# Both exponentials of a batch together, consumers later, four h banks and a shorter prologue in a fused attention and snake kernel

## Chip, cores, metric

One core of a Trainium2 chip. Times are device microseconds (us) of a whole execution; a profile's span, from its first to its last instruction, is 1.5 to 2 us shorter. The kernel before takes 348.2 us (median of three runs, 345.6 to 351.0).

## The reference

```python
# attention part: x (8, 8, 512, 64), state (8, 8, 32, 64), B, H, S, D = x.shape
a  = softmax(x @ state^T / sqrt(D));      xread = a  @ state   # (8, 8, 512, 64)
a2 = softmax(state @ x^T / sqrt(D));      sread = a2 @ x       # (8, 8,  32, 64)
h_in = concat([xread, sread], axis=2) -> (4352, 512)
# MoE part: w_in (512, 2048), w_out (2048, 512), alpha (2048)
h = h_in @ w_in;  s = sin(alpha * h);  g = h + s * s / (alpha + 1e-9);  out = g @ w_out
```

## The kernel before

A pass `t` has 16 slots `f`, one for each 128 rows of the hidden layer. A slot makes `h` of batch `t` (`mm1`: 2 matmuls, a sine on ScalarE, its square on GpSimd; in pass 0 every second square is on VectorE), finishes the slot before it (`snake` on VectorE: `g = h + s2 / alpha`), does a quarter of an output tile of batch `t-1` (`mm2`: 4 matmuls), and one step of the attention of batch `t+1` (the list `fill`). Pass 8 treats the state rows. M is state times w_in, so that `h = A @ M`. There are eight PSUM banks: 3 for h, 2 for the output, 3 (`psX`, "px") for all the rest.

```python
psH = tile_pool(name="psH", bufs=3, PSUM); psO = (bufs=2); psX = (bufs=3)
...
load_x(0, 2); ... w_in (4 loads); load_x(1, 1); w_out (4 loads)
for b in range(2, B):
    load_x(b, 1)                      # all issued by GpSimd (POOL) at the start
...
def s_step(ii):                       # scores of two of four row blocks, and their exponential
    ... 8 matmuls into sp ...
    nc.scalar.activation(a.E[:, 2*ii:2*ii+2, :], sp[:], ACT.Exp, scale=scale)
def r_step(ii):                       # row sums, reciprocal (VectorE); normalise (GpSimd)
    nc.vector.reduce_sum(R, E8, axis=AX.X); nc.vector.reciprocal(rR, R)
    nc.gpsimd.tensor_tensor(A8, E8, rR..., ALU.mult)
def a_step(): ...                     # transposes of A; copy to AT (needed by mm1 of the next pass)
...
return [lambda: t_step(0),            # pack (VectorE) and transposes of x
        lambda: t_step(1), lambda: s_step(0),
        lambda: (s_step(1), r_step(0)), lambda: r_step(1), None, a_step]
...
fill = [an[0], an[1], an[2], an[3], an[4], mn[0], an[6]] + mn[1:]   # mn: eight M steps
fill = fill + w_steps(t)              # W and C (the state rows' attention): slots 14, 15
for f in range(FT):
    cur = mm1(t, f)
    if fill[f]: fill[f]()
    if pend: snake(*pend)             # one slot behind
    pend = (t, f) + cur
    if t > 0: mm2(t - 1, f // 4, (f % 4) * 4, (f % 4) * 4 + 4, box)
```

The softmax here doesn't subtract the row's maximum and nothing guards it: scores larger than these inputs give would overflow.

## Time and profile before

| | before |
|---|---|
| time, us | 348.2 (345.6 to 351.0) |
| TensorE busy, share of the span | 78% |
| mean granted TensorE clock | 0.879 |
| table loads on ScalarE | 30, of 1.28 us |
| prologue / t=0 / passes t=1..6 / rest, us | 33.4 / 33.9 / 226.1 / 54.3 |

The last row cuts the span at the first transposes of a batch, the group whose output is `x_ps`; the rest is t=7, t=8 and the last output tiles. The lines are in the prediction. The clock of the prologue is not to be trusted: the profile gives 1.00 there, before the first change that it recorded.

### The profile page before, as it was taken

To read this page: it belongs to the slowest core of one execution; us is meant where nothing else is said; L and a number is where in the kernel's file an instruction comes from. 1 tells how busy PE (TensorE), PEld (TensorE's weight loads), DVE (VectorE), ACT (ScalarE), POOL (GpSimd) and SP (SyncE) were. 2 spreads that over 40 slices of the span, in tenths; PEclk is the share of its full clock that TensorE was granted. 3 is DMA by queue.
4 is the path that set the end of the run, shared out by engine and by line. 5 is a ranking of instruction groups with operands and counts; after the bars stand their busy time and mean duration, and the time that the engine had idled before them with its cause. 6 is when DMAs were issued, how large, how long until landed. Compare 5 with 4: busy or idle time off the path is not lost.

```text
span 347.7 us, 4220 instructions
## 1 busy us (share of the span) xinstructions
PE 269.5 (78%) x1536; PEld 119.7 (34%) x1536; DVE 178.1 (51%) x285; ACT 174.5 (50%) x256; POOL 165.3 (48%) x176
## 2 busy tenths in 40 slices
PE   2515478695997689776979599749978699999993
PEld 1302222342343233332334234313333235445651
DVE  3522666744466346754565355744654466654320
ACT  1212955266452935384635745493528464564431
POOL 8433342226462465345552646345534556785420
PEclk9999855587898969996998789987989699999998
DMA  8999960000000000000110000000000001011112
GB/s 105 206 203 203 197 83 1 2 1 31 30 32 30 30 32 30 30 2 30 38 55 0 31 30 32 30 31 32 30 32 1 30 32 61 30 62 53 38 62 61
DMA packets 19780, 17.84 MB, mean 51 GB/s; under 512 B 2992, under 2 KB 15280, under 8 KB 19760
## 3 DMA queue, kind: packets, MB, share of 16 engines
q0 software_dynamic: 12704, 8.65, 16.7%
q1 hardware_dynamic: 7056, 8.92, 7.3%
q8 instruction: 12, 0.20, 0.3%
q14 instruction: 8, 0.07, 0.1%
HBM read 17.31 MB, written 8.91 MB: 75 GB/s over the span
## 4 chain that ended last, share of the span: by engine, by line
PE 56%; ACT 15%; DVE 9%; issue 7%; POOL 6%; DMA 5%; ACTq 0%; POOLq 0%
PE o_ps L309 30%; PE h_ps L282 13%; ACT L293 5%; DMA w_out_sb<-in_moe_w_out_dram 5%; PE m_ps L218 5%; ACT L176 4%; ACT s L293 4%; PE x_ps L158 3%; POOL A L185 3%; DVE xp L146 3%; DVE gT L300 2%; PE h_ps L288 2%; DVE rC L264 2%; PE a_ps L193 2%; ACT o_sb L315 1%
## 5 line engine op out<-in xcount | busy, mean ns | idle before, releaser
L296 POOL TENSOR_TENSOR s<-s 128x512 bf16<-128x512 bf16 (+1 forms) x136 | 134.2, 989 | 153.0 <-ACT s L293 147.3
L293 ACT ACTIVATE s<-h_ps,alpha_sb 128x512 bf16<-128x512 f32 (+1 forms) x144 | 94.9, 664 | 118.6 <-PE h_ps L282 107.7
L309 PE MATMUL o_ps<-w_out_sb,gT 128*128 128x512 bf16 x544 | 149.3, 402 | 0.0
L300 DVE SCALAR_TENSOR_TENSOR gT<-s,inva_sb,h_ps 128x512 bf16<-128x512 bf16 (+1 forms) x144 | 100.7, 705 | 37.3 <-POOL s L296 36.4
L282 PE MATMUL h_ps<-AT,M 128*128 128x512 bf16 x256 | 87.2, 426 | 20.6 <-DVE gT L300 20.6
L309 PEld LDWEIGHTS <-gT 128*128 128x128 bf16 x544 | 49.2, 102 | 56.1 <-issue 19.6
L282 PEld LDWEIGHTS <-M 128*128 128x128 bf16 x256 | 25.8, 104 | 57.2 <-issue 34.8
L228 DVE CAST M<-m_ps 128x512 bf16<-128x512 f32 x32 | 22.0, 687 | 34.3 <-PE m_ps L218 34.3
L315 ACT COPY o_sb<-o_ps 128x512 f32<-128x512 f32 x34 | 19.9, 584 | 21.4 <-PE o_ps L309 20.9
L218 PE MATMUL m_ps<-w_in_sb,stT 128*64 128x512 bf16 x128 | 29.9, 479 | 0.2 <-ACT M L226 0.2
L193 PE MATMUL a_ps<-ident,A 128*128 128x128 bf16 x64 | 9.5, 301 | 24.8 <-POOL A L185 24.8
L158 PE MATMUL x_ps<-ident,xp 128*128 128x128 bf16 x128 | 13.2, 265 | 19.7 <-DVE xp L146 19.7
L226 ACT CAST M<-m_ps 128x512 bf16<-128x512 f32 x32 | 18.6, 580 | 13.5 <-PE m_ps L218 13.5
L183 DVE TENSOR_REDUCE R<-E 128x16 f32<-128x512 bf16 x16 | 11.0, 684 | 26.7 <-ACT E L176 26.6
L158 PEld LDWEIGHTS <-xp 128*128 128x128 bf16 x128 | 10.5, 121 | 27.1 <-DVE xp L146 24.4
L176 ACT ACT_TABLE_LOAD x15 | 19.2, 1283 | 1.0 <-PEq L378 0.7
L163 DVE COPY xT<-x_ps 128x1024 bf16<-128x1024 bf16 x16 | 11.1, 691 | 16.5 <-PE x_ps L158 16.5
L293 ACT ACT_TABLE_LOAD x15 | 19.2, 1283 | 0.3
L185 POOL TENSOR_TENSOR A<-E,rR 128x512 bf16<-128x512 bf16 x16 | 16.9, 1059 | 4.3 <-DVE rR L184 4.3
L218 PEld LDWEIGHTS <-stT 128*64 128x64 bf16 x128 | 7.6, 115 | 31.1 <-issue 30.9
L193 PEld LDWEIGHTS <-A 128*128 128x128 bf16 x64 | 6.3, 134 | 30.4 <-POOL A L185 27.5
L176 ACT ACTIVATE E<-s_ps 128x512 bf16<-128x512 f32 x16 | 9.4, 597 | 13.5 <-PE s_ps L170 13.3
(33 smaller groups left out, 110.7 us busy)
## 6 DMA issues: line engine op xcount, KB each, us to landing
out_dram<-o_sb SPq DMA_DIRECT2D x32, 256.0 KB, 2.2
xnat<-in_x_dram POOLq DMA_DIRECT2D x7, 512.0 KB, 21.2
w_in_sb<-in_moe_w_in_dram POOLq DMA_DIRECT2D x4, 512.0 KB, 10.2
w_out_sb<-in_moe_w_out_dram POOLq DMA_DIRECT2D x4, 512.0 KB, 19.2
xnat<-in_x_dram POOLq DMA_DIRECT2D x2, 256.0 KB, 5.5
out_dram<-o_sb SPq DMA_DIRECT2D x8, 64.0 KB, 1.7
st_nat<-in_state_dram POOLq DMA_DIRECT2D x1, 256.0 KB, 4.5
alpha_sb<-in_moe_alpha_dram SPq DMA_DIRECT2D x1, 8.0 KB, 3.1
```

Of the source, the lines that this page charges most:

```text
L158: nc.tensor.transpose(tp[:, k, i * P:(i + 1) * P], a.xp[:, i, 2 * q:2 * q + 2, :].rearrange("p r d -> p (r d)"), ident[:],)
L176: nc.scalar.activation(a.E[:, 2 * ii:2 * ii + 2, :], sp[:], ACT.Exp, scale=scale)
L185: nc.gpsimd.tensor_tensor(A8, E8, rR.unsqueeze(2).to_broadcast([P, 2 * H, Ns]), ALU.mult)
L193: nc.tensor.transpose(tp[:, g, i * P:(i + 1) * P], a.A[:, i, g * P:(g + 1) * P], ident[:],)
L218: nc.tensor.matmul(mp[k * 2 * Ns:(k + 1) * 2 * Ns, :], stT[:, b * G + g, k * 2 * Ns:(k + 1) * 2 * Ns], w_in_sb[:, q, fs * FW:(fs + 1) * FW ...
L228: nc.vector.tensor_copy(dst, mp[:])
L282: nc.tensor.matmul(hp[:, :n], Ms[t][:, g, f * P:(f + 1) * P], atts[t].AT[:, g, :], start=(g == 0), stop=(g == G - 1),)
L293: nc.scalar.activation(s[:, :n], hp[:, :n], ACT.Sin, scale=alpha_sb[:, f:f + 1])
L296: eng.tensor_tensor(s2[:, :n], s[:, :n], s[:, :n], ALU.mult)
L300: nc.vector.scalar_tensor_tensor(gT[t][:, f, :n], s2[:, :n], inva_sb[:, f:f + 1], hp[:, :n], ALU.mult, ALU.add)
L309: nc.tensor.matmul(op[:], gT[t][:, ft, st * P:(st + 1) * P], w_out_sb[:, ft, :], start=(ft == 0), stop=(ft == FT - 1),)
L315: nc.scalar.copy(o_sb[:], op[:])
```

## The change

Its intent is to keep TensorE from waiting in a pass, and to start earlier. The exponentials of a batch stand together (two table loads a pass instead of four); their consumers come some slots later; four h banks and a snake two slots behind give slack; W and C move from slots 14 and 15 to 6 and 7; the pack moves from slot 0 to the end of the slot before it; inputs of later batches are loaded two passes ahead instead of all at the start; the state is transposed with half the matmuls; twelve matmuls on zeros are to warm the clock. In pass 0 all squares go to GpSimd and all copies of M to ScalarE, and W and C share one bank. In the diff, T are the transposes of x, S the scores, X the exponential, Rs the row sums and reciprocal, N the normalisation, AT_ the transposes of A; the pack is the copy of x into `xp` that T needs.

```diff
-    psH bufs=3 ... psX bufs=3          (sinp bufs=3)
+    psH bufs=4 ... psX bufs=2          (sinp bufs=4)
-    for b in range(2, B):
-        load_x(b, 1)
... (prologue)
+    warm_up(12)
     prep_state()                        # 16 transposes of doubled columns instead of 32
+    a.S(0); a.X(0); a.S(1); a.X(1); <load the sine table>; a.Rs(0); a.N(0, nc.gpsimd)
+    a.Rs(1); a.N(1, nc.vector); m_step(0, 0..3, True); a.AT_([0]); a.AT_([1])
+    m_step(0, 4..7, True); atts[1] = Att(1); atts[1].pack(0, 1)
... (a pass)
-        fill = [an[0], an[1], an[2], an[3], an[4], mn[0], an[6]] + mn[1:]
+            add(pe, 0, n.T, 0);  add(pe, 1, n.T, 1)
+            add(pe, 3, n.S, 0);  add(pe, 4, n.S, 1)
+            add(post, 4, n.X, 0); add(post, 4, n.X, 1)
+            add(post, 7, n.Rs, 0)
+            add(post, 8, n.N, 0, nc.gpsimd); add(post, 8, n.Rs, 1)
+            add(post, 9, n.N, 1, nc.gpsimd)
+            add(pe, 12, n.AT_, [0, 1])
+            for k, s in enumerate((2, 8, 9, 10, 11, 13, 14, 15)):
+                add(pe, s, m_step, t + 1, k, t == 0 or k % 2 == 0)
+            s = 6 if t + 1 < B else 0
+            add(pe, s, atts[t].W); add(pe, s + 1, atts[t].Cs)
+            add(post, 5, load_x, t + 2, 1)
+            add(post, 15, nxt)            # pack of batch t + 2
-        eng = nc.vector if (t == 0 and f % 2) else nc.gpsimd; eng.tensor_tensor(s2 ...)
+        nc.gpsimd.tensor_tensor(s2 ...)
-            if pend: snake(*pend)
+            pend.append((t, f) + cur)
+            if len(pend) > LAG: snake(*pend.pop(0))      # LAG = 2
```

`pe` work goes ahead of the slot's snake and mm2, `post` work behind them. A half batch is now four heads of all rows instead of all heads of half the rows, which changes no size.

## The prediction

> **What bounds the kernel now.** I read the page's forty slices first, then the windows table cut at the kernel's own stages, then the timeline of one steady period and of the start.
>
> ```profile
> PE   2515478695997689776979599749978699999993
> ...
> PEclk9999855587898969996998789987989699999998
> ```
>
> TensorE (PE) is the busiest engine, but it has dips at regular distances, and in the same slices the granted clock falls to 5 to 8 tenths. So there is a periodic hole, and after each hole TensorE runs slowly. I cut the span where the first transposes of a batch start (the x_ps group of the timeline): 33.4, 67.3, 106.9, ... 257.2, and at 293.4, where t=7 begins, which has none. The columns are: stretch, its length, then busy us (instructions) of PE, PEld, DVE, ACT, POOL, then the clock, DMA share and GB/s.
>
> ```profile
> 0.00:33.40 33.40, 11.15 (x90) 6.20 (x91) 12.02 (x26) 5.79 (x8) 17.05 (x26) 1.00 1.18 178
> 33.40:67.32 33.92, 23.07 (x113) 8.26 (x113) 22.04 (x38) 19.82 (x28) 11.54 (x11) 0.62 0.59 80
> ...
> 182.10:220.20 38.10, 31.38 (x177) 13.43 (x178) 20.66 (x31) 20.96 (x30) 18.55 (x18) 0.87 0.08 28
> ...
> 293.40:347.70 54.30, 48.55 (x269) 24.99 (x266) 22.04 (x37) 23.24 (x42) 26.42 (x32) 0.98 0.16 54
> ```
>
> These are the prologue (33.4 us), the pass t=0 (33.9), one of the six steady passes t=1..6 (67.3 to 293.4 us, so 226.1 in all, 37.7 each), and t=7, t=8 and the drain (54.3). In a steady pass TensorE is busy 31.4 of 38.1 us at clock 0.87; ACT, DVE and POOL are at about 21, 21 and 19 us, none near the bound. In the last stretch TensorE is 48.6 of 54.3 busy at 0.98. So TensorE bounds the end, and in the steady passes it is TensorE plus holes and cold clock. The holes, from the timeline (start, length, engine, line; in brackets idle before and what ended it):
>
> ```profile
> 180.51 1.53 DVE L146 COPY xp<-xnat 128x2048 bf16<-128x2048 bf16 x1
> ...
> 182.10 1.03 PE L158 MATMUL x_ps<-ident,xp 128*128 128x128 bf16 x8 [2.51 <-DVE xp L146]
> ...
> 187.99 1.28 ACT L176 ACT_TABLE_LOAD   x1
> ...
> 189.29 0.60 ACT L176 ACTIVATE E<-s_ps 128x512 bf16<-128x512 f32 x1
> ...
> 189.90 1.28 ACT L293 ACT_TABLE_LOAD   x1
> ...
> 191.90 1.28 ACT L176 ACT_TABLE_LOAD   x1
> ...
> 193.20 0.60 ACT L176 ACTIVATE E<-s_ps 128x512 bf16<-128x512 f32 x1
> ...
> 194.29 1.28 ACT L293 ACT_TABLE_LOAD   x1
> ...
> 194.72 0.66 DVE L300 SCALAR_TENSOR_TENSOR gT<-s,inva_sb,h_ps 128x512 bf16<-128x512 bf16 x1
> 195.43 1.01 PE L282 MATMUL h_ps<-AT,M 128*128 128x512 bf16 x2 [2.01 <-DVE gT L300]
> ...
> 198.44 0.82 PE L193 MATMUL a_ps<-ident,A 128*128 128x128 bf16 x6 [1.79 <-POOL A L185]
> ```
>
> The first pair: the transposes of the next batch waited 2.51 us for its pack copy. The rest: ScalarE (ACT) switches table four times, 1.28 us each, because each of the two exponentials stands between sines; the sines come late, h banks come free late (TensorE idle 2.01 us for gT), and then the a_ps transposes wait 1.79 us for POOL's normalisation. Idle here is 38.10 - 31.38 = 6.7 us. At the start:
>
> ```profile
> 16.91 0.88 POOL L77 DMA_DIRECT2D xnat<-in_x_dram  x1 [1.66 <-DMA w_in_sb<-in_moe_w_in_dram]
> ...
> 22.11 0.88 POOL L77 DMA_DIRECT2D xnat<-in_x_dram  x1 [1.74 <-DMA xnat<-in_x_dram]
> ...
> 27.19 0.87 POOL L77 DMA_DIRECT2D xnat<-in_x_dram  x1 [1.67 <-DMA w_out_sb<-in_moe_w_out_dram]
> 28.08 2.06 POOL L185 TENSOR_TENSOR A<-E,rR 128x512 bf16<-128x512 bf16 x2
> ...
> 30.20 0.82 PE L193 MATMUL a_ps<-ident,A 128*128 128x128 bf16 x6 [0.60 <-POOL A L185]
> ```
>
> POOL is stuck issuing input loads: each of the last ones waits for an older transfer, 2.5 us apart, so POOL's first normalisation starts only at 28.08, and everything else waits for it.
>
> **What the Trainium skill says.** "TensorE: Matmul & The Clock Gate", Part 1 and "HAM oscillation": half rate by default, full rate after some 3.4 us of sustained work, back to half after an idle window of that length. The trace agrees in kind: in 1 us windows the clock was 0.50 from 182 to 185 and back at 1.00 by 186, after a hole of 2.5 us, so the hole can be shorter than the page's rule; after the same hole at 217.7 it did not fall.
> "ScalarE: Activation LUTs", What ACT_TABLE_LOAD costs: about 1283 ns, plus a drain, about 2.66 us a switch. The trace agrees on 1283 ns but shows no drain: sine and table load, and load and exponential, follow each other within 0.02 us. I use 1.28.
> "PSUM — Partial Sum Buffer", Specifications: 8 banks. Both kernels use all: 3+2+3 before, 4+2+2 after.
> "SBUF — State Buffer", Who interferes with whom: copies in VectorE's two-port mode and GpSimd block each other. The trace fits: the same 128x2048 pack copy took 0.68 us at 32.7 us, between POOL instructions, and 1.53 beside them. I use 1.5 in a steady pass.
>
> **The change, part by part.**
> *Dense cost of a steady pass.* The TensorE work is unchanged. Of the chain of waits, one slot (mm1 2 matmuls, mm2 4) takes 1.30 us when dense (300 to 320 us) and 1.74 with an M step (92 to 98 us). From distances in the timeline at full clock: a group of x transposes 0.46, a group of eight scores 0.23, A transposes 0.46 (estimated as eight x transposes), all W 0.46, C 0.34. Sum: 16 x 1.30 + 8 x 0.44 + 2 x 0.46 + 2 x 0.23 + 0.46 + 0.46 + 0.34 = 20.8 + 3.5 + 2.6 = 27.0 us. Against 38.1 there are 11.1 us to win: 6.7 idle, and 0.13 x 38.1 = 5.0 of clock.
> *Both exponentials together.* Two table loads instead of four. Take the end of mm1 of slot 4 as zero: sine at 0.8, load 2.1, exponentials 2.7 and 3.3, load 4.6, sine 5 at 5.3, its square on POOL at 6.4, snake at 7.2. With four h banks mm1 of slot 9 is the first to need that snake. Slots 5 to 8 give TensorE 4 x 1.3 plus W 0.46, C 0.34 and an M step 0.44, plus the rest of slot 4, so it comes there at about 7.5: hidden, just. VectorE then has in a row C's reciprocal and products (0.96 + 0.59), snakes, two reductions with reciprocals (2 x 0.94) and M copies; snake 6 ends near 9.7 against 9.2 wanted. I take 0.8 us of stalls here.
> *Consumers later.* The normalisations are in slots 8 and 9, A transposes in slot 12: by the same count POOL ends at 12.7, TensorE arrives at 13.5. The 1.8 us wait goes.
> *Pack.* The new order puts the pack behind the M copy and snake of slot 15, and its transposes into the next slot. From the end of the last M matmul: copy 0.8, snake 1.55, pack 3.1; TensorE has mm2 0.86 and mm1 0.43, so it waits 1.8 us. The hole shrinks from 2.5 but stays.
> *Clock.* One 1.8 us hole and some small ones; I allow a fall after a third of the holes, 3.3 us at half rate, and a little more: 0.6 us. Sum of a pass: 27.0 + 0.8 + 1.8 + 0.6 = 30.2, I take 30.
> *t=0.* There is no mm2 to cover the table loads. From the first T: TensorE at half rate for slots 0 to 4 (5 x 0.85 + T, S and one M step) about 7 us; sine 5 is ready 5.3 later and slot 9 starts 7.2 later, at about 14; from there POOL sets the pace with seven squares and two normalisations at 1.05, and the last M steps and pack follow: about 26.5 (now 33.9).
> *Prologue.* Twelve loads instead of eighteen before POOL's first normalisation; the last of them was issued at 11.8 in the old run, so POOL is free by 12.6, and the chain (state transposes halved, eight M copies on ACT, 8 x 0.58, from about 15.4) brings mm1 to about 20.5. But the pack of batch 1 waits for its load: the old POOL issue at 22.11 was released by that landing, so the first T is at about 23 (now 33.4). The 12 warm-up matmuls (estimated 0.43 each, 5 us) run while the state is still loading, so they cost nothing; TensorE idles again after them, and I give them no gain.
> *End.* 54.3, unchanged: already dense.
> Sum: 23 + 26.5 + 6 x 30 - 2 (the sixth pass packs nothing) + 54.3 = 281.8. **Predicted: 282 us**, 19% less.
>
> **Rivals.**
> *The clock stays low.* If the 1.8 us hole and the small ones still bring half rate for 8 us in each pass, a pass is 33 to 34: 303 us. For it: a 2.5 us hole was enough in several passes, and t=0 before stayed at 0.50 through 48 to 72 us although TensorE was 80 to 100% busy. Against: slots 1 to 4 and 11 to 15 have nothing to wait for.
> *In-order queues and two px banks.* W in slot 6 takes the bank of the first scores and waits for the exponential; VectorE's run of ten instructions after slot 7 delays snakes and so mm1. By my count slack is only 0.3 to 0.6 us. If each slips by one slot, two more stalls of 1.5 us a pass: 33, total 300.
> *The gain is only at the start.* If the DMA of inputs sets it, the prologue keeps most of its time: 8 us worse, 290. For: 205 GB/s flows throughout the first 40 us.
> *Everything hides.* If the pack overlaps (0.7 us instead of 1.5) and the clock stays full: passes of 28, 268 us.
>
> **Range and chances.** Passes of 28.5 to 32 move the sum by -9 and +12, t=0 and prologue by 4 or so together; the runs before spread over 345.6 to 351.0. Surprises lie mostly on the slow side. Range 272 to 298. Even rivals one and two together leave about 320, still 8% faster, so faster 0.97, same 0.02, slower 0.01.
>
> **What would show it.** Right: ACT table loads fall from 30 to 16 (one pair for each of batches 1 to 7, and one at the start); in steady passes TensorE busy above 90% with clock above 0.93 and the wait of L282 for gT under 1 us a pass; distance between first transposes of a batch about 30 us; one remaining wait of x_ps for xp of about 1.8 us a pass; first T of batch 1 near 23 us. Wrong: passes above 32 with PEclk under 0.9 (rival one), long waits of PE for snakes, E or px banks in slots 6 to 11 (rival two), or first T later than 28 us (rival three).

## The result

The changed kernel takes 277.43 us (277.06 to 277.65, four runs) against 349.2 (345.56 to 350.99) of the kernel before. The ratio is 0.797, interval 0.790 to 0.804. A ratio here is the mean time of one kernel's fast runs over that of the other's of the same rounds, so not quite the ratio of the medians. Predicted: 282, range 272 to 298.

The page of the changed kernel, the busy tenths of TensorE and its granted clock in 40 slices:

```profile
PE   7568565899989998999899989999999999999991
...
PEclk9955979599999999999999999999999999999998
```

Against the same lines of before, the regular dips are gone, and the clock falls only in the first quarter. The windows, cut as before (length; busy of PE, PEld, DVE, ACT, POOL; clock; DMA share; GB/s):

```profile
0.00:22.31 22.31, 14.39 (x85) 6.40 (x86) 10.22 (x20) 10.21 (x17) 11.50 (x20) 0.82 1.13 167
22.31:49.14 26.83, 17.66 (x111) 7.65 (x113) 17.99 (x25) 17.94 (x28) 19.90 (x20) 0.82 0.57 87
49.14:80.30 31.16, 29.82 (x172) 13.29 (x177) 19.42 (x31) 18.18 (x28) 18.22 (x18) 0.90 0.23 44
80.30:108.59 28.29, 27.26 (x174) 11.98 (x177) 19.42 (x31) 18.20 (x29) 19.26 (x19) 1.00 0.26 56
```

The prologue is 22.3 us (11.1 less), t=0 26.8 (7.1 less), t=1 to t=6 together 172.5 (221.6 - 49.14, so 53.6 less), the rest, from 221.60, 54.3 (the same). That is the whole difference of the spans, 347.7 - 275.9 = 71.8. A steady pass is 28.29 us with TensorE busy in all but about 1 us and the clock at 1.00. Table loads on ScalarE are 16 instead of 30.

How the exponentials now stand in a pass, from the timeline (start, length, engine, line):

```profile
88.03 1.28 ACT L189 ACT_TABLE_LOAD   x1
...
89.32 1.08 ACT L189 ACTIVATE E<-s_ps 128x512 bf16<-128x512 f32 x2
...
89.97 0.63 PE L216 MATMUL w_ps<-E,xp 128*128 128x64 bf16 x16
...
90.42 1.28 ACT L279 ACT_TABLE_LOAD   x1
...
91.72 1.84 ACT L279 ACTIVATE s<-h_ps,alpha_sb 128x512 bf16<-128x512 f32 x3
```

The gap for sines on ScalarE is 3.7 us (88.03 to 91.72), but TensorE goes on with mm1, W and mm2 and waits for nothing. At the end of a pass one wait is left:

```profile
79.43 0.81 DVE L158 COPY xp<-xnat 128x2048 bf16<-128x2048 bf16 x1
...
80.30 0.62 PE L170 MATMUL x_ps<-ident,xp 128*128 128x128 bf16 x8 [0.77 <-DVE xp L158]
```

The pack took 0.81 us and not 1.5, because it ran mostly in a gap of POOL's squares (79.70 to 80.39 here), so TensorE waited 0.77 us. At the end of t=0 POOL has no gap, and the same copy took 2.85 us and ended 0.6 us after the last square; TensorE waited 3.17 us, and the clock was 0.50 until 55 us:

```profile
46.24 2.85 DVE L158 COPY xp<-xnat 128x2048 bf16<-128x2048 bf16 x1
...
49.14 1.03 PE L170 MATMUL x_ps<-ident,xp 128*128 128x128 bf16 x8 [3.17 <-DVE xp L158]
```

And the prologue ends where the load of batch 1 lands:

```profile
21.56 0.69 DVE L158 COPY xp<-xnat 128x2048 bf16<-128x2048 bf16 x1 [4.28 <-DMA xnat<-in_x_dram]
...
22.31 1.03 PE L170 MATMUL x_ps<-ident,xp 128*128 128x128 bf16 x8 [1.30 <-DVE xp L158]
```

### The profile page after: what moved, and what is told of

Read it like the earlier page. It is cut to its first block, busy times and chain, and to the rows that moved or that the text cites. A ratio compares the mean times of both kernels' runs of the same rounds, so it can differ in the third digit from the quotient of the medians.

```text
span 275.9 us, 4169 instructions
## 1 busy us (share of the span) xinstructions
PE 246.4 (89%) x1504; PEld 112.7 (41%) x1532; DVE 166.2 (60%) x267; ACT 160.5 (58%) x254; POOL 171.5 (62%) x183
## 4 chain that ended last, share of the span: by engine, by line
PE 68%; DVE 17%; DMA 5%; POOL 4%; issue 3%; ACT 1%; ACTq 0%; POOLq 0%
PE o_ps L294 36%; PE h_ps L268 16%; DVE gT L285 6%; DMA xnat<-in_x_dram 5%; PE m_ps L250 5%; PE x_ps L170 3%; DVE rC L234 3%; DVE xp L158 3%; PE h_ps L274 3%; DVE M L260 2%; POOL s L281 2%; DVE xs_all L237 2%; PE w_ps L216 2%; DVE R L193 2%; PE s_ps L180 1%
## 5 line engine op out<-in xcount | busy, mean ns | idle before, releaser
L281 POOL TENSOR_TENSOR s<-s 128x512 bf16<-128x512 bf16 (+1 forms) x144 | 141.6, 992 | 89.3 <-ACT s L279 89.0
L294 PE MATMUL o_ps<-w_out_sb,gT 128*128 128x512 bf16 x522 | 136.5, 383 | 1.2 <-issue 0.7
L268 PE MATMUL h_ps<-AT,M 128*128 128x512 bf16 x250 | 77.6, 392 | 5.8 <-DVE gT L285 4.3
L268 PEld LDWEIGHTS <-M 128*128 128x128 bf16 x256 | 24.8, 100 | 36.4 <-issue 11.2
L250 PE MATMUL m_ps<-w_in_sb,stT 128*64 128x512 bf16 x128 | 27.6, 433 | 3.2 <-ACT M L258 1.6
L258 ACT CAST M<-m_ps 128x512 bf16<-128x512 f32 x40 | 22.8, 580 | 2.6 <-PE m_ps L250 2.6
L260 DVE CAST M<-m_ps 128x512 bf16<-128x512 f32 x24 | 16.2, 674 | 10.6 <-PE m_ps L250 10.6
L234 DVE RECIPROCAL rC<-w_ps 128x128 f32<-128x128 f32 x8 | 7.7, 958 | 17.3 <-PE w_ps L227 17.3
L210 DVE COPY AT<-a_ps 128x1024 bf16<-128x1024 bf16 (+1 forms) x9 | 5.7, 633 | 9.4 <-PE a_ps L207 9.3
L193 DVE TENSOR_REDUCE R<-E 128x16 f32<-128x512 bf16 x16 | 10.8, 676 | 0.5 <-ACT E L189 0.5
L158 DVE COPY xp<-xnat 128x2048 bf16<-128x2048 bf16 (+1 forms) x9 | 8.6, 959 | 4.3 <-DMA xnat<-in_x_dram 4.3
L274 PE MATMUL h_ps<-xs_all,w_in_sb 128*128 128x256 bf16 x64 | 9.6, 273 | 0.0
```

The source lines that it names most:

```text
L158: nc.vector.tensor_copy(a.xp[:, :, hs, :], xnat_l[a.b][:, hs, :].rearrange("p h (i d) -> p i h d", i=C),)
L250: nc.tensor.matmul(mp[h * 2 * Ns:(h + 1) * 2 * Ns, :], stT[:, b * G + g, h * 2 * Ns:(h + 1) * 2 * Ns], w_in_sb[:, 2 * g + h, fs * FW:(fs + ...
L258: nc.scalar.copy(dst, mp[:])
L260: nc.vector.tensor_copy(dst, mp[:])
L268: nc.tensor.matmul(hp[:, :n], Ms[t][:, g, f * P:(f + 1) * P], atts[t].AT[:, g, :], start=(g == 0), stop=(g == G - 1),)
L274: nc.tensor.matmul(hp[:, :n], w_in_sb[:, q, f * P:(f + 1) * P], xs_all[:, q, :], start=(q == 0), stop=(q == Q - 1),)
```

## The experiments

Twelve kernels, all correct. Names with u_ undo one part of the changed kernel; b_ put a part into the kernel before; p_ go further. Most were looked at once (the profiled run, whose state is unknown with one run); their steady passes repeat within 0.1 us wherever the clock stays up, so I compare passes (distance between first x transposes) and use the time only for large differences. Three calls ran on three chips; before had medians 349.65 (seven runs), 347.36 (one run) and 347.89 us (seven) on them.

| run | time, us | passes from t=1 to t=5, us | first T of batch 1 at, us |
|---|---|---|---|
| before | 348.2 | 39.6, 38.2, 37.1, 38.1, 37.0 | 33.4 |
| changed | 277.4 | 31.2, then 28.29 | 22.3 |
| u_exp | 294.2 | 32.3, then 30.75 | 23.0 |
| u_early | 279.2 | 30.4, then 28.92 | 22.5 |
| u_h3lag1 | 288.2 | 31.9, then 30.20 | 22.7 |
| u_wc | 291.2 | 32.4, 31.4, 31.3, 29.7, 31.4 | 23.2 |
| u_warm | 276.1 | 30.8, then 28.29 | 22.2 |
| u_load | 280.5 | 28.3, then 28.29 | 33.1 |
| b_exp | 321.8 | 33.0, 33.0, 33.8, 33.7, 34.7 | 33.7 |
| b_bank | 351.0 | 40.0, 38.2, 37.1, 38.1, 37.0 | 34.1 |
| b_late | 335.1 | 36.2, 34.8, 36.4, 34.7, 34.8 | 33.6 |
| b_all | 307.4 | 32.4, 31.0, 32.6, 31.0, 31.0 | 33.8 |
| p_pack | 271.6 | 27.8, then 27.34 | 22.7 |
| p_best | 268.1 | 27.34 throughout | 19.5 |

### Undoing one part of a pass

**u_exp**, the exponentials apart:

```diff
-            add(post, 4, n.X, 0)
+            add(post, 3, n.X, 0)
```

> The changed kernel with the first exponential of a batch moved back to slot 3, so that a sine stands between the two and a pass has four table loads again instead of two. Theory (waits hidden by slack): sine 4 comes 3.2 us later and sine 5 about 1.8 us after the time at which TensorE wants its bank, so a pass grows from 28.3 by 1.5 to 2.5 us, TensorE waits for gT in slots 8 to 10, clock stays near 1.0, time 286 to 293 us. Rival (clock): the wait brings half rate and passes go to 33 or more, time over 305. Rival (table loads off the path anyway): no change, 277.

Measured: passes 30.75, 2.46 us more, clock 1.00 in them; table loads 30 again. The wait for gT over the whole kernel, from the list of waits (total us, times, longest), in the changed kernel and in u_exp:

```profile
PE h_ps L268 <- DVE gT L285: 4.3, 5, 2.1
```

```profile
PE h_ps L268 <- DVE gT L285: 19.4, 17, 2.5
```

15.1 us more, over about seven passes: the mechanism and the size of a pass are as the theory had them. The time, 294.2 us, lies just above the range of 286 to 293.

**u_early**, consumers directly behind the exponentials:

```diff
-            add(post, 7, n.Rs, 0); add(post, 8, n.N, 0, nc.gpsimd)
-            add(post, 8, n.Rs, 1); add(post, 9, n.N, 1, nc.gpsimd)
-            add(pe, 12, n.AT_, [0, 1])         # M steps: 2, 8, 9, 10, 11, 13, 14, 15
+            add(post, 4, n.Rs, 0); add(post, 4, n.N, 0, nc.gpsimd)
+            add(post, 5, n.Rs, 1); add(post, 5, n.N, 1, nc.gpsimd)
+            add(pe, 8, n.AT_, [0, 1])          # M steps: 2, 9, 10, 11, 12, 13, 14, 15
```

> The changed kernel with the consumers put back early: reductions and normalisations in slots 4 and 5 directly behind the exponentials, A transposes in slot 8 instead of 12. Theory: TensorE comes to slot 8 about 1.2 us before POOL has the second normalisation, so a pass grows by about 1.2 us to 29.5 and the wait is of a_ps for A; time about 285. Rival (clock): passes over 31 with clock under 0.95. Rival (lateness of consumers does nothing): 277.

Measured: passes 28.92, 0.63 more, with a wait of 0.5 us of a_ps for A. The place is right, the size half of what I said: with the slack of the banks, lateness matters little. t=0 was 1.4 us shorter (25.5), so the time moved by 1.8 us only.

**u_h3lag1**, three h banks, three px banks, one slot behind:

```diff
-    psH bufs=4, psX bufs=2, LAG = 2
+    psH bufs=3, psX bufs=3, LAG = 1
```

> The changed kernel with three h banks and three px banks and the snake one slot behind, as before the change. Theory: mm1 of slot 8 instead of slot 9 is the first to need the snake of slot 5, so TensorE waits about 1 us there and 0.6 us in each of the next two; passes 30.5, wait of h_ps for gT about 2.2 us a pass, time about 290. Rival (clock): passes 33. Rival (banks do nothing): 277.

Measured: passes 30.20, 1.91 more; in a pass TensorE waited for gT 1.22, 0.38 and 0.18 us. Right in mechanism and size. The clock stayed at 1.00, so the rival falls. (The h banks, the px banks and the distance of the snake are not separated.)

**u_wc**, W and C back to the end of the pass:

```diff
-            s = 6 if t + 1 < B else 0          # M steps: 2, 8, 9, 10, 11, 13, 14, 15
+            s = 14 if t + 1 < B else 0         # M steps: 2, 6, 7, 8, 9, 10, 11, 13
```

> The changed kernel with W and C back in slots 14 and 15 and the M steps in slots 6 to 13. Theory: C's reciprocal and products (1.55 us on VectorE) then stand ahead of the snake and the pack at the end of a pass, so the wait of the transposes for the pack grows from 0.77 to about 2.5 us as in the kernel before; passes 30.0 if the clock holds, up to 31.5 if it falls after the hole; time 287 to 297. Rival (place of W and C does nothing): 277.

Measured: mean 31.2. Four of the five pack holes were followed by a stretch of 3.4 us at half rate; the pass without one took 29.7 us, the three others from t=2 on 31.3 to 31.4, so a fall costs 1.7 us. From its timeline:

```profile
109.65 0.96 DVE L234 RECIPROCAL rC<-w_ps 128x128 f32<-128x128 f32 x1 [1.53 <-PE w_ps L227]
...
110.64 0.59 DVE L237 TENSOR_TENSOR xs_all<-w_ps,rC 64x128 bf16<-64x128 f32 x2
...
111.26 0.75 DVE L285 SCALAR_TENSOR_TENSOR gT<-s,inva_sb,h_ps 128x512 bf16<-128x512 bf16 x1
...
111.93 1.51 DVE L158 COPY xp<-xnat 128x2048 bf16<-128x2048 bf16 x1
...
113.50 0.71 PE L170 MATMUL x_ps<-ident,xp 128*128 128x128 bf16 x5 [2.51 <-DVE xp L158]
```

VectorE works through C's reciprocal and products (109.65 to 111.23), a snake and the pack in one row, and the transposes wait 2.51 us, to the hundredth what they waited in the kernel before. So the hole that the prediction put down to the pack's place alone is C's doing: in u_wc the pack still has its new place, and the hole is as long as in the old one. VectorE's order there is even that of the kernel before (reciprocal 178.24, products 179.23, snake 179.85, pack 180.51): behind C, the end of slot 15 and the start of slot 0 are the same place in its queue. (The M steps moved with W and C, which is not separated.)

### One part alone in the kernel before

**b_exp** takes the exponentials out of `s_step` and issues both in slot 3, before `r_step(0)`:

```diff
-            lambda: (s_step(1), r_step(0)),
+            lambda: (s_step(1), x_step(0), x_step(1), r_step(0)),
```

> The kernel before with one part alone: both exponentials of a batch together in slot 3, two table loads a pass instead of four. Theory (the parts need each other): sine 4 is now held 3.8 us in one piece, the second normalisation stands on POOL behind its square, and the A transposes still come in slot 6, so TensorE waits there about 2.9 us instead of 2.0 for gT and 1.8 for A; idle of a pass 5.4 instead of 6.7 us, passes 36 to 37 (now 37.7), time 338 to 346. Rival (the table loads are the whole matter): passes lose the two loads and the cold clock after them, 33 to 34, time about 325.

**b_bank**:

```diff
-    psH bufs=3, psX bufs=3, sinp bufs=3; snake one slot behind
+    psH bufs=4, psX bufs=2, sinp bufs=4; snake two slots behind
```

> The kernel before with four h banks, two px banks and the snake two slots behind, nothing else. Theory: the wait for gT goes, but TensorE then only comes earlier to the A transposes in slot 6, whose data hang on the same table loads; passes 37 to 38, time 345 to 350, wait of a_ps for A grows to about 4 us a pass. Rival (banks are the matter): passes 34, time 327.

Measured: 351.0 us, 1 us above the range. That banks alone do nothing is as expected, but the reason is not: over the five passes the wait for gT did not go (12.1 us, 12.0 before) and the wait for A did not grow (10.6, 10.5 before). By the code, mm1 still needs a snake that was issued two slots before it: with three banks and one slot behind, and with four and two.

**b_late**:

```diff
-            fill = [an[0], an[1], an[2], an[3], an[4], mn[0], an[6]] + mn[1:]
+            fill = [t0, t1, s0, s1, m0, m1, m2, (r0, m3), r1, m4, m5, a, m6, m7]   # + W, C
```

> The kernel before with only the consumers later: reductions and normalisations in slots 7 and 8, A transposes in slot 11, M steps moved forward into slots 4 to 7. Theory: the wait for A (1.8 us) goes, the wait for gT (2 us) and the pack hole (2.5 us) stay, the clock rises a little; passes 34.5 to 36.5, time 329 to 341. Rival: the DVE and POOL queues only move the wait, 37.5, time 348.

Measured: 335.1 us, in the range. Over the five passes the wait for A (10.5 us) is gone, and the wait for gT grew from 12.0 to 15.5.

**b_all** is the three together.

> The kernel before with all three: exponentials together, consumers later, four h banks with the snake two slots behind. The old prologue, the old place of the pack (slot 0) and of W and C (slots 14, 15) stay. Theory: only the pack hole of 2.5 us and 0.5 us of small waits stay, and the clock falls after some of the pack holes; passes 30.5 to 32, more gained than the sum of the three runs alone, time about 306 to 313. Rival (clock): the pack hole alone keeps the clock at 0.87 and passes at 33.5 or more, time over 323.

Means of the five passes: 38.0 before, b_exp 33.6, b_bank 38.1, b_late 35.4, b_all 31.6. The differences are -4.3, +0.1 and -2.6, sum -6.8; together -6.4. So the parts add to within 0.4 us (one run each), and my theory that together they gain more than the sum is refuted. In b_all a wait of 1.2 us a pass came in that none of the parts had: M's matmuls for a px bank that an exponential had to free. The banks do depend on the rest: nothing here, 1.9 us a pass in the changed kernel (u_h3lag1, where the snake and the px banks changed with them). The windows over these five passes, of before and b_exp:

```profile
67.32:257.21 189.89, 154.78 (x881) 66.28 (x881) 103.13 (x155) 104.83 (x150) 92.75 (x90) 0.88 0.08 28
```

```profile
64.64:232.85 168.21, 140.82 (x865) 62.54 (x881) 101.82 (x155) 92.07 (x140) 93.28 (x90) 0.97 0.09 32
```

Idle time (length less PE busy) is 7.0 us a pass before and 5.5 in b_exp, nearly the 5.4 that I expected (16 matmul records of b_exp are missing, so it is at most 5.5). What I left out is the second figure: PE busy falls from 31.0 to 28.2 us a pass, because the clock rises from 0.88 to 0.97. Cut into half microseconds, the windows show where: in the kernel before each of these five passes has a stretch of 6.8 us at 0.50 in its middle (195.3 to 202.1, for one). Two holes lie there about 1 us apart, of 2.0 us for gT and of 1.8 to 2.3 us for A. The stretch begins at the end of the first (at 195.3, 0.1 us before it is over) or at most 0.4 us into the second, so it is the first hole that brings it; with the second in it, it lasts 6.8 us and not 3.4. In b_exp, where the holes are 1.9 and at most 1.1 us, one pass of five has it, for 3.4 us. The rival was nearer in its number (33 to 34), though more by the clock than by the length of the loads.

What decides about the clock can be read off the traces. In all 14 of them every stretch between two changes of the clock is a whole multiple of 3.41 us. Cut on this grid, after the first 28 us of a trace, all 43 windows at full clock in which TensorE idled 2.05 us or more were followed by half rate, none of the 896 with less than 1.6 us, and 15 of the 36 between. So the same pack hole counts differently by how it lies on the grid. In the kernel before:

```profile
178.24:181.65 3.41, 1.35 (x6) 0.39 (x4) 3.33 (x5) 1.34 (x3) 2.08 (x2) 1.00 0.22 82
...
215.79:219.20 3.41, 1.87 (x19) 0.76 (x15) 2.82 (x5) 1.86 (x3) 1.98 (x3) 1.00 0.14 53
```

The hole before 182.10 puts 2.06 us of idle into one window, and the clock was 0.50 from 181.65. The hole before 220.17, just as long, is cut into 1.54 and 0.97 us, and the clock stayed at 1.00.

### The start, and further

**u_warm** drops `warm_up(12)`.

> The changed kernel without the twelve warm-up matmuls. Theory: the prologue's chain runs up to 2 us slower at half rate, but the first transposes of batch 1 wait for the load that lands at 21.5 us, so the time is the same within 1 us: 277. Rival (warm-up shortens the start): 279 to 282, first transposes of batch 1 later than 24 us.

Measured: 276.11 us (274.41 to 277.11, four runs), ratio to before 0.787 (0.783 to 0.791) where the changed kernel has 0.797 (0.790 to 0.804). First T at 22.2 instead of 22.3, passes the same. The twelve matmuls did raise the rate (sixteen transposes of x took 1.18 us in the changed kernel, 1.89 here), but the first T waits for the load of batch 1 in both. The warm-up gains nothing; whether it costs a microsecond is not settled, as the two were not run in the same rounds.

**u_load** issues all loads at the start again:

```diff
+    for b in range(2, B):
+        load_x(b, 1)
-            add(post, 5, load_x, t + 2, 1)       # xpool: B buffers instead of 3
```

> The changed kernel with the loads of batches 2 to 7 issued at the start again, behind the weights, instead of two passes ahead. Theory: POOL is held by the issue of loads until about 28 us as before the change, so its normalisation, the A transposes and the first transposes of batch 1 come about 10 us later (32 to 33 instead of 22.3); passes unchanged at 28.3; time 286 to 289. Rival (the shorter transposes, ScalarE's M copies and the order of the prologue make the gain, not the loads): first transposes of batch 1 by 25 us, time under 281.

Measured: first T at 33.1 us, as the theory said. From its timeline, POOL's last load issue and the first A transposes:

```profile
26.74 0.88 POOL L76 DMA_DIRECT2D xnat<-in_x_dram  x1 [1.67 <-DMA w_out_sb<-in_moe_w_out_dram]
27.64 1.06 POOL L202 TENSOR_TENSOR A<-E,rR 128x512 bf16<-128x512 bf16 x1
...
28.75 1.03 PE L210 MATMUL a_ps<-ident,A 128*128 128x128 bf16 x8 [13.46 <-POOL A L202]
```

But the time is only 280.5. The span grew by 2.8 us: +10.8 in the prologue, -5.0 in t=0 and -2.9 in t=1. Here is t=0 of u_load, to be held against 22.31:49.14 of the changed kernel above:

```profile
33.07:54.90 21.83, 16.16 (x114) 6.63 (x112) 15.91 (x25) 18.32 (x29) 17.70 (x18) 0.90 0.93 126
```

Its clock is 0.90 instead of 0.82: full rate came about 1 us after the first T instead of 5.5 (that the transposes and M steps close together just ahead of it did this is argued, not shown). And its pack took 0.85 us instead of 2.85, so t=1 began warm. So the deferral of the loads is what moves the start, and nearly three quarters of that is given back in t=0 and t=1. The pack did not fall into a gap: POOL's squares stand back to back in both runs, and the pack started 0.3 us before the end of one in both. Here the copy came first, and the next square took 1.48 us instead of 1.04:

```profile
53.99 0.85 DVE L161 COPY xp<-xnat 128x2048 bf16<-128x2048 bf16 x1
...
54.25 1.48 POOL L284 TENSOR_TENSOR s<-s 128x512 bf16<-128x512 bf16 x1
```

It was likewise in u_h3lag1 (0.92, beside a square of 1.42); in the changed kernel, u_exp, u_early and u_warm the copy took 2.85 and ended after the last square. No run shows what decides it. TensorE waited 1.17 us for it here and 3.17 there; with the cold start of t=1 that followed there (2.9 us), about 4.9 of the 7.9 us given back hang on the order of two instructions and not on the loads.

**p_pack**, the pack in slot 12:

```diff
-            add(post, 15, nxt)
+            add(post, 12, nxt)
```

> The changed kernel with the pack of the batch after next in slot 12 instead of 15. Theory: no wait of x_ps for xp in any pass: 0.77 us less in each of five and 3.2 us less at the end of pass t=0, and without that last hole the clock does not fall at the start of t=1, about 2 us more; time 267 to 271. Rival (the pack beside POOL's squares takes up to 2.9 us wherever it stands and delays the snakes): 275 to 278.

Measured: 271.61 us (271.18 to 271.76), ratio 0.781 (0.775 to 0.787). Steady passes 27.34 with no wait for xp, 0.95 less, and t=1 27.8 instead of 31.2. The time is 0.6 us above the theory's range, because t=0 kept its hole: the pack now took 3.79 us beside five squares in a row and held the snakes, so there the rival was right:

```profile
41.27 5.02 POOL L281 TENSOR_TENSOR s<-s 128x512 bf16<-128x512 bf16 x5
...
43.06 3.79 DVE L158 COPY xp<-xnat 128x2048 bf16<-128x2048 bf16 x1
...
47.55 1.01 PE L268 MATMUL h_ps<-AT,M 128*128 128x512 bf16 x2 [3.43 <-DVE gT L285]
```

**p_best**: pack in slot 12; no warm-up; batch 1 loaded ahead of the last two quarters of w_in, whose M steps move into t=0; four of t=0's squares on VectorE.

```diff
+        if k == 2: load_x(1, 1)                   # inside the loop of w_in loads
+        eng = nc.vector if (t == 0 and f in (9, 11, 13, 15)) else nc.gpsimd
+                for k, s in ((4, 2), (5, 2), (6, 8), (7, 9)):
+                    add(pe, s, m_step, 0, k, True)    # in t == 0; batch 1's steps from slot 10
```

> A version from what was learnt: pack in slot 12; no warm-up; the load of batch 1 ahead of the last two quarters of w_in, whose M steps move into pass t=0; four squares of t=0 on VectorE. Theory: first transposes of batch 1 at about 17.6 us instead of 22.3 (4.7 less), t=0 about 3 us shorter, pack and clock as in the run beside it (9 less): 259 to 264. Rival (VectorE or ScalarE becomes the bound of t=0): no gain there, 264 to 267.

Measured: 268.14 us (267.25 to 268.61), ratio 0.771 (0.766 to 0.776), 23% faster than before and 3% than the changed kernel. First T at 19.5 instead of 22.3; the rest of the expected start did not come, and t=0 stayed at 27.9 us. The time is above the ranges of the theory (259 to 264) and of the rival (264 to 267). The rival was right that t=0 gains nothing, but not in the reason: of the four squares on VectorE three took 0.42 us, and one, beside instructions of POOL back to back until 37.47, took 3.68 and held the snakes behind it, so that TensorE waited 3.57 us for gT:

```profile
34.07 3.68 DVE L283 TENSOR_TENSOR s<-s 128x512 bf16<-128x512 bf16 x1
```

## Why the prediction was right

- **Prologue**, predicted 23, measured 22.3. The last load issue of POOL (11.54), mm1 at about 20.4 and the wait for batch 1's load came as worked out. What the step did not say is that most of this time is given back later, a good part of it by the order of two instructions (u_load).
- **t=0**, 26.5, measured 26.8: half rate at first, then POOL at one square in 1.04 us. The sum is luck in part: from slot 9 on POOL had thirteen instructions in a row (35.5 to 48.5) and not nine, while the M steps and the pack, put at some 3 us behind them, took 0.6.
- **Passes t=1 to t=6**, 178, measured 172.5. This is the term that was mis-sized. *Dense cost* 27.0: p_pack's passes, busy 99.6% at full clock, take 27.34, so the sum of slots was right to 1%. *Stalls behind the exponentials* 0.8: about 0.2 (28.29 - 27.34 - 0.77). *Pack* 1.8: 0.77, since I took the copy's 1.5 us from a pass where POOL held it up and it had 0.81 here. *Clock* 0.6: none in t=2 to t=6, but 2.9 us in t=1 after the 3.17 us hole, which the prediction missed because it took the pack in t=0 to be as in the other passes.
- **End**, 54.3, measured 54.3.
- **Sum** 281.8 against 275.9 of the span: it is a sum of stretches of the span, so the 1.8 us between span and time were left out of the 282. Slips that change nothing: 6.7 and 5.0 us make 11.7 and not the 11.1 to win; passes of 28 give about 270 and not 268; and TensorE was not 80 to 100% busy throughout 48 to 72 us, it idled 2.5 us before 67.32.
- **Rivals.** The clock staying low did not happen in steady passes: with holes of 0.77 us it is 1.00. Two px banks and in-order queues cost at most 0.2 us in a steady pass; in t=0 of p_pack and p_best the queues did cost 3.4 and 3.6. The start-only rival is wrong: 53.6 of 71.8 us come from the passes.
- **Reasons that fell.** "The hole shrinks because the pack comes earlier": u_wc shows that it shrinks because C left: with C ahead of it the hole is as long in the new place. And the 5.0 us of clock per pass I put on holes in general; the runs show that most of it belonged to the middle of the pass (6.8 us at half rate, in all five), and to the pack hole 3.4 us at half rate in three passes of five.

## What to carry to other kernels

Work out what the critical engine needs when it never waits; p_pack shows that such a sum can be right to 1%, and then only the remaining holes have to be found. A hole costs its length and, where it puts 2.05 us or more of idle into one of the 3.41 us windows, the clock after it too (43 of 43 here; 0 of 896 under 1.6 us); a hole of 2.0 to 2.5 us did so or not by how it lay. So a part of a change that shortens holes below that earns more than their idle time. Behind every hole look at the in-order queue of the engine that ends it, for what stood ahead (C's reciprocal), and at what ran beside it on POOL (a copy of 0.69 us took up to 3.79).

## What the Trainium skill lacked or had wrong

- "ScalarE: Activation LUTs", What ACT_TABLE_LOAD costs: the load of 1283 ns is as measured, but of the drain of about 1380 ns the trace shows nothing: the table load at 88.03 us ends at 89.31 and the exponential starts at 89.32.
- "TensorE: Matmul & The Clock Gate", Part 1: it gives an idle window of about 3.4 us for the fall. Here single holes of 2.5 us were followed by half rate in 3 of 5 passes of the kernel before, 4 of 5 of u_wc and 1 of 5 of b_all, holes of 2.0 us with one of about 2 us close behind in 5 of 5, and holes of 0.77 us in none of 5; what counted was 2.05 us or more of idle in a window of 3.41 us (43 of 43), not a window idle throughout. The page does not say how busy an engine must be to be warmed: from 46 to 66 us the kernel before had PE busy 16.0 of 20.0 us and stayed at 0.50 throughout.
- "SBUF — State Buffer", Who interferes with whom: it says that the one that comes first holds the shared ports for its whole instruction. The runs show a VectorE copy that is late by more than one GpSimd instruction: the pack of 0.69 us alone took 2.85 and 3.79 us beside back-to-back squares of 1.04 us (and 0.85 in u_load, where the square took 1.48). The page has no figure for such a queue.
